# Attention and gated feed-forward on one core: a step's output weights, the next block's queries and a load of h asked for at other places

## The chip, the cores and the metric

The kernel runs on one core of one Trainium2 chip, in one launch. The time is device microseconds (us) of that core, from three runs: 851.23, 847.15 and 847.97, median 847.97. Engines are named as the profile names them: PE (TensorE matmul), PEld (its weight load), DVE (VectorE), ACT (ScalarE), POOL (GpSimd), and SP, which here issues nearly all DMAs from one queue in program order.

## The reference

What is computed is attention within chunks of 64 positions, then a gated feed-forward layer on all tokens:

```python
# q, k, v: (8, 8, 576, 64); chunk 64
scores = scale * np.matmul(q_c, k_c.transpose(0, 1, 2, 4, 3))
scores = scores - np.max(scores, axis=-1, keepdims=True)
attn = np.exp(scores)
attn = attn / (np.sum(attn, axis=-1, keepdims=True) + 1e-09)
out = np.matmul(attn, v_c)
# x: (4608, 512) out of the heads; w_gate, w_val: (512, 1536); w_out: (1536, 512)
g = x @ w_gate
silu = g * (1.0 / (1.0 + np.exp(-g)))
val = x @ w_val
return (silu * val @ w_out).astype(np.float32)
```

All arrays are float32.

## The kernel before

The 4608 tokens are nine blocks of 512 (`N`), and the 1536 inner columns twelve steps of 128 (`NF`). A float32 factor is split into an upper and a lower part, and a product is three matmuls: lower by upper, upper by lower, upper by upper. So a step of one block is 12 matmuls for the gate, 12 for the value, and 12 for the projection with the output weights (`project`, L583 to L585). `lag` puts each projection one step behind, so that its factors (`hh` cast by ACT, `hl` subtracted by DVE, both in `split`, L70 and L71) have a step's time to be made.

The stages that matter here, with their place in the span:

- Up to about 181 us, blocks 0 and 1 go through `first_seven`, which makes the two blocks' gates and values with seven products instead of eight (L915). Block 1's inner values h are kept in HBM for later. Its last call is step 11. After it the next block (`nxt`, the third one) has its scores made, in two halves (L307), and the loads of block 1's h begin (`fetch_h`, L1008).
- From 181 to about 217 us a loop over f projects block 1's steps from what `fetch_h` brings. Beside it goes the third block's attention.
- From 217 to about 325 us a loop over i (twelve steps, f = i + 4 modulo 12) does the third block's feed-forward, with 24 matmuls by `gated` (L505) and 12 by `project` in each step. Beside it, blocks 4 and 5 have their attention done, and six sums of output weights are made, which later blocks use (`WeightSums`): a load of raw weights (`qk_t<-r`, L1403), three POOL subtractions (L1406 to L1408), an ACT cast (L1412), two POOL subtractions (L1415), two stores (`sums<-qk_t`, L1419).
- After that, pairs of blocks.

The order of PE, ACT and DVE is the order of the code (`tc.manual_schedule`), and POOL's is too in the loop over i. So each of these engines stands still until the wait at the head of its queue is over, whatever else would be ready. SP's order is the code's up to the first scores; later a scheduler sets it, which a call `tc.issue_after(x)` holds back until after instruction x. `recent[0]` is the latest load of output weights (`out_again`). The sums' load stands under it:

```python
def sums(self):
    with tc.issue_after(recent[0]):
        nc.sync.dma_start(out=self.raw, in_=kept_raw[self.j].rearrange("p i m -> p (i m)"))
```

`begin_sums(1)` is called at the end of `behind[2]`, that is after step i = 2; `weight_sums[1].split()`, with the ACT cast, stands in `middle[3]`, between step i = 3's gate and value and the cast of its `hh`. What ACT has to do next after that `hh` is to copy the scores of block 4 out of the two PSUM banks of the pool `ps_gv` (L315). The pool has two buffers only: step i = 4's gate and value go to the same two banks.

Of the kernel before, what the change touches and what calls it, by code (L numbers as in the profile page):

```python
# [24 lines left out]
NF = DF // P  # L25
# [8 lines left out]
def attn_then_gated_ffn(ctx: ExitStack, tc: tile.TileContext, qk, v, wgv, wo, out):  # L34
    nc = tc.nc
    const = ctx.enter_context(tc.tile_pool(name="const", bufs=1))
# [7 lines left out]
    ps_gv = ctx.enter_context(tc.tile_pool(name="ps_gv", bufs=2, space=bass.MemoryType.PSUM))  # L44
# [140 lines left out]
    SEVEN, EARLY = 5, 4  # L185
# [29 lines left out]
    def save_w(f):  # L215
        kept_w[f] = store.tile([P, 2, 4 * Q], F32, name=f"w{f}")
        nc.sync.dma_start(out=kept_w[f], in_=w_both[f].bitcast(F32))
# [290 lines left out]
    def out_weights(f, engine=None):  # L508
        both = wp.tile([P, 2, DM], F32R, name="both", tag="wo")
        split(wo_raw[f], both[:, 0], both[:, 1], engine)  # L510
        if f % 2 == 0:
            o = store.tile([P, 2, 2, DM], F32, name=f"o{f}")
            kept_o[f], kept_o[f + 1], two_o[f // 2] = o[:, 0], o[:, 1], o
        out_now[f] = both
        return both[:, 0], both[:, 1]
# [3 lines left out]
    def save_o(f):  # L519
        nc.sync.dma_start(out=kept_o[f], in_=out_now[f].bitcast(F32))  # L520
        if f % 2 == 0:
            kept_raw.append(store.tile([P, 2, DM], F32, name=f"r{f}"))
        nc.sync.dma_start(out=kept_raw[f // 2][:, f % 2], in_=wo_raw[f])
# [3 lines left out]
    def out_again(f, pool=wp, tag="wo"):  # L527
        both = pool.tile([P, 2, DM], F32R, name="both", tag=tag)
        recent[:] = [nc.sync.dma_start(out=both.bitcast(F32), in_=kept_o[f]).ins]
        return both[:, 0], both[:, 1]  # L530
# [87 lines left out]
    def put_off(h):  # L618
        f = len(waiting)
        if f % 2 == 0:  # L620
            kept_h.append(store.tile([P, 2, N], F32, name=f"h{f}"))
        waiting.append(kept_h[-1][:, f % 2])
        nc.scalar.dma_start(out=waiting[f], in_=h)
# [44 lines left out]
    class Product:  # L668
# [4 lines left out]
        def add(self, *which):  # L673
            for w in which:
                self.left -= 1
                some(self.ps, *self.at, [w], first=self.left == 3 * NK - 1, last=not self.left)
# [126 lines left out]
    wo_f = out_weights(0)  # L803
# [56 lines left out]
    for f in range(1, SEVEN):  # L860
# [32 lines left out]
        if f + 1 in (2, SEVEN):  # L893
            quarters = Quarters(f + 1, "w6" if f == 1 else None)
            quarters.sums(w.t)
        up[f + 2].scale()
        wo_f = out_weights(f)
# [12 lines left out]
    def seventh(ps, x, factors, i, first):  # L910
        which, q = FACTORS[i]
        w = [t.rearrange("p (i k m) -> p i k m", i=4, m=P)[:, q] for t in factors[which]]
        for k in range(NK // 2):
            for n, (u, v) in enumerate(((0, 1), (1, 0), (0, 0))):
                nc.tensor.matmul(ps, w[u][:, k], in_turn(x[i][v][:, k]), start=first and k == 0 and n == 0,  # L915
                                 stop=k == NK // 2 - 1 and n == 2, skip_group_check=True)
# [4 lines left out]
    def turns(which):  # L921

        if pending:
            project(*pending[0], which=which)
            if T - 1 in which:
                pending.pop()

    def first_seven(f, done, before):

        o, w = down[f], up[f + 1] if f + 1 < NF else None  # L930
        if f + 2 < NF:
            up[f + 2].load()
        save_o(f - 1)
        done.save()
        if f == NF - 2:
            save_w(EARLY)
            save_w(EARLY + 1)
        factors = (w_both[f][:, 0], w_both[f][:, 1]), done.halves

        def product(ps, i, first):  # L940
            seventh(ps, x_first, factors, i, first)

        ps1 = ps_a.tile([P, N], F32, name="ps_a", tag="ps_a")
        ps2, ps3 = (ps_gv.tile([P, N], F32, name="ps_gv") for _ in range(2))
        h = hp.tile([P, N], F32, name="h")
        v1, v2 = (ld.tile([P, N], F32, name="v", tag="v_t") for _ in range(2))
        product(ps1, 0, True)
        if w:
            w.below()
            w.shift()  # L950
        if f + 1 < NF:
            down[f + 1].load()
        nc.scalar.copy(out=h, in_=ps1)
        o.below()
        if f < NF - 1:
            put_off(before)
        product(ps2, 1, True)
        if w:
            w.join()
            w.upper()  # L960
        nc.scalar.copy(out=v2, in_=ps2)
        turns([0])
        product(ps1, 2, False)
        quarters = Quarters(f + 1)
        if w:
            quarters.sums(w.t)
            w.lower()
        nc.scalar.copy(out=v1, in_=ps1)
        if w:
            quarters.upper()  # L970
        o.shift()
        o.join()
        product(ps3, 3, True)
        add(h, ps3)
        if w:
            quarters.lower()
        nc.scalar.activation(h, h, AF.Silu, scale=2.0 ** -8)
        turns([1])
        product(ps1, 4, False)
        add(v2, ps1)  # L980
        wo_f = out_weights(f, nc.gpsimd)
        product(ps2, 5, False)
        if f + 2 < NF:
            up[f + 2].scale()
        if f + 1 < NF:
            down[f + 1].scale()
        add(v1, ps2)
        times(h, v1)
        p = parts(a0, f, h)
        turns([2])  # L990
        product(ps1, 6, False)
        h2 = const.tile([P, N], F32, name="h2", tag="ts") if f == NF - 2 else hp.tile([P, N], F32, name="h")
        nc.scalar.activation(h2, ps1, AF.Silu, scale=2.0 ** -8)
        turns([3])
        times(h2, v2)
        pending.append((p, wo_f))
        return quarters, h2

    for f in range(SEVEN, NF - 1):
        quarters, h1 = first_seven(f, quarters, h1)  # L1000


    late, last_fetch = [], []

    def fetch_h(i):
        if i < NF // 2 - 1:
            h = ld.tile([P, 2, N], F32, name="h_in", tag="qk_t")
            last_fetch[:] = [nc.sync.dma_start(out=h, in_=kept_h[i]).ins]  # L1008
            late.append(h)
# [9 lines left out]
    def fetch_o(n):  # L1019
        while len(ready_o) < min(n, NF - 2):  # L1020
            f = len(ready_o)
            ready_o.append(out_again(f, const, f"wo{f % 5 - 1}") if f % 5 in (1, 2) else out_again(f))


    nxt = First(2)
    a1.steps = NF - 2, NF - 3
    last_o = pending[0][1]
    _, h2 = first_seven(NF - 1, quarters, None)
    first_qk = [nxt.load_qk(0), nxt.load_qk(1)], [nxt.load_qk(2, 2, const, "turned")]
    fetch_o(2)  # L1030
    nxt.less_top(nxt.products(first_qk[0], ps_gv, "ps_gv"), 0)
    fetch_h(0)
    put = [(parts(a1, NF - 2, h1), last_o)]
    wo_f = pending[0][1]
    lag(None, None)
# [398 lines left out]
    a, pair = nxt, []  # L1434
# [13 lines left out]
    in_order.__enter__()  # L1448
    for f in range(NF):
        lag(*put.pop(0))  # L1450
        fetch_o(f + 3)
        extra.get(f, lambda: None)()
        if f == 7:
            late_sums[EARLY].begin("w3", copied[0])
        elif f == 10:
            late_sums[EARLY].split()
        if f + 2 < NF:
            put.append((prepare(f), ready_o[f]))
        if f == 9:
            with tc.issue_after(recent[0]):  # L1460
                save_w(EARLY + 2)

    pair = pair[0]
    c = pair.a[0]
# [8 lines left out]
    def load_late(a, after):  # L1473
        with tc.issue_after(after):
            load_values(a)
# [12 lines left out]
        with tc.issue_after(weight_sums[3].stored):  # L1488
            scores(a)

    late_queries = []

    def load_second():
        late_queries.append([pair.second().load_qk(0, 2, const, moved(0))])
# [4 lines left out]
    t1, t2 = Turns(c), Turns(None)  # L1499

    def some_of_second(n):
# [4 lines left out]
              4: lambda: pair.a[1].exponents(0, NP), 5: lambda: some_of_second(4), 6: lambda: some_of_second(4),  # L1506
              7: lambda: some_of_second(4)}
    behind = {0: lambda: (c.normalize(0, NP), t1.some(2)), 1: lambda: (load_second(), load_second_too(), t1.some(10)),
              2: lambda: (t1.some(6), load_late(c, pair.a[1].asked)),
              3: lambda: scores(pair.a[1], False, late_queries),  # L1510
              4: lambda: (cross(c, False), pair.a[1].normalize(0, NP)), 5: lambda: some_of_second(10),
              6: lambda: (some_of_second(10), load_late(pair.a[1], weight_sums[2].stored)), 7: lambda: (pair.x0(), pair.x3()),
# [16 lines left out]
    for i in range(NF):  # L1529
        f = (i + EARLY) % NF  # L1530
        h = gated(a, f)
        middle.get(i, lambda: None)()
        wo_f = out_again(f)
        lag(parts(a, f, h), wo_f)
        with tc.issue_after(recent[0]):
            if i in TILES_AGAIN:
                again(TILES_AGAIN.index(i))
            if i in STORED:
                save_w(EARLY + 3 + STORED.index(i))
        if i in SAVED:  # L1540
            late_sums[SAVED[i]].save()
        if i == 4:
            late_sums[0].begin(("ts", "wo0"), pair.a[1].exponentials)
        elif i == 5:
            late_sums[1].begin(moved(5))
        elif i == 6:
            late_sums[1].split()
        behind[i]()
    in_order.__exit__(None, None, None)
    for b in range(3, NB, 2):  # L1550
        pair.last = b + 2 == NB
        middle, beside, behind, bursts, later = {}, {}, {}, {}, {}
        if not pair.last:
            n = Pair(b + 2, moved(11))
            c = n.a[0]
            bursts = {0: lambda: late_scores(c), 3: lambda: scores(n.second()), 8: lambda: cross(c), 10: lambda: cross(n.a[1])}
            middle = {2: lambda: c.exponents(0, NP), 5: lambda: n.a[1].exponents(0, NP), 10: lambda: load_late(n.a[1], asked_left[0]), 11: lambda: (n.s1(), n.s4())}
            t1, t2 = Turns(c), Turns(None)
# [19 lines left out]
        if not pair.last:  # L1578
            pair = n
# [34 lines left out]
```

## Time and profile before

| | before |
|---|---|
| median of three runs | 847.97 us |
| the profiled execution, its own time | 848.97 us |
| its span, first to last instruction | 847.2 us |
| PE busy | 829.5 us, 98% |
| DVE, ACT, POOL busy | 606.3, 433.6, 161.8 us |
| DMA, mean over the span | 273 GB/s |
| mean granted TensorE clock | 0.999 |

Busy time of an engine counts its instructions alone, not what it waits for. With PE busy 98% of the span, some 17.7 us are left in which it is not; which of them a change can reach is read from PE's waits in the stretch in question. A share of the whole span says little on such a stretch. A DMA's time runs from its issue to its landing, and holds what it waits behind in the queue.

### The profile page before, as it was taken

What the parts mean: (1) busy time and instruction counts of PE and PEld (TensorE: products, weight loads), DVE (VectorE), ACT (ScalarE), POOL (GpSimd) and SP (SyncE); (2) the same over time, 40 slices, a digit from 0 to 9 for tenths busy, and PEclk for the clock granted to TensorE, in tenths of its full rate; (3) what the DMA queues carried; (4) which work ended last, traced back from release to release, by engine and by line L of the source; (5) the groups of instructions that cost most, each with busy time, mean ns of one, the idle gap of its engine ahead of it and who ended that gap; (6) DMA issues with size and microseconds to landing.
All of it is one profiled execution on the core that took longest, in us unless ns stands there. A gap on an engine that the chain in (4) does not pass through costs nothing.

```text
span 847.2 us, 16691 instructions
## 1 busy us (share of the span) xinstructions
PE 829.5 (98%) x6689; PEld 742.8 (88%) x6689; DVE 606.3 (72%) x946; ACT 433.6 (51%) x650; POOL 161.8 (19%) x118
## 2 busy tenths in 40 slices
PE   7999999999999999999999999999999999999997
PEld 6788888878887888888889998888889988888997
DVE  5898988854798956568886976678768943333475
ACT  4876889753625345535335743553337533333353
POOL 1300001102155742233110001413010002222100
PEclk9999999999999999999999999999999999999999
DMA  9698788899999899866678779666768576666643
GB/s 351 250 337 310 291 297 315 322 336 303 411 326 360 298 406 373 299 212 227 234 256 303 265 231 335 233 209 227 233 208 298 163 259 231 230 227 226 241 173 114
DMA packets 96654, 231.27 MB, mean 273 GB/s; under 512 B 32064, under 2 KB 58176, under 8 KB 83904
## 3 DMA queue, kind: packets, MB, share of 16 engines
q1 hardware_dynamic: 94848, 227.31, 75.3%
q10 hardware_dynamic: 1728, 2.88, 1.1%
q8 instruction: 53, 0.87, 0.4%
q14 instruction: 25, 0.20, 0.1%
HBM read 177.21 MB, written 52.95 MB: 272 GB/s over the span
## 4 chain that ended last, share of the span: by engine, by line
PE 86%; DMA 7%; POOL 2%; DVE 2%; ACT 1%; issue 1%; SPq 0%; DVEq 0%; ACTq 0%; POOLq 0%
PE ps_a L915 26%; PE ps_gv L915 19%; PE ps_o L571 14%; PE ps_gv L505 10%; PE ps_gv L571 6%; DMA v_t<-in_v 3%; PE ps_o L583 2%; PE ps_o L584 2%; PE ps_o L585 2%; PE ps_a L307 2%; DMA qk_t<-r 1%; PE ps_a L395 1%; DMA h_in<-h 1%; DMA both<-o 1%; POOL qk_t L1406 1%
## 5 line engine op out<-in xcount | busy, mean ns | idle before, releaser
L915 PE MATMUL ps_a<-x,factors 128*128 128x512 f32 x864 | 211.1, 380 | 0.4 <-issue 0.4
L915 PEld LDWEIGHTS ps_a<-x,factors 128*128 128x128 f32 x864 | 154.3, 190 | 18.1 <-issue 1.1
L915 PE MATMUL ps_gv<-x,factors 128*128 128x512 f32 x648 | 157.6, 379 | 0.1
L915 PEld LDWEIGHTS ps_gv<-x,factors 128*128 128x128 f32 x648 | 122.3, 189 | 17.9 <-PE ps_a L915 0.4
L1240 POOL TENSOR_TENSOR kept<-kept 128x512 f32<-128x512 f32 x39 | 57.0, 1460 | 362.8 <-DVE kept L555 358.5
L505 PE MATMUL ps_gv<-xh,w 128*128 128x512 f32 x352 | 103.3, 380 | 0.0
L382 DVE STREAM_TRANSPOSE turned<-s_sb 32x256 f32<-32x256 f32 x192 | 83.7, 436 | 3.1
L70 ACT CAST hh<-kept 128x512 fp32r<-128x512 f32 x111 | 67.2, 617 | 28.7 <-PE ps_o L571 15.4
L505 PEld LDWEIGHTS ps_gv<-xh,w 128*128 128x128 f32 x352 | 66.4, 189 | 9.4 <-ACT xh L660 0.2
L1214 ACT ACTIVATE kept<-ps_a 128x512 f32<-128x512 f32 x36 | 21.5, 598 | 89.7 <-PE ps_a L915 89.3
L505 PE MATMUL ps_gv<-xl,w 128*128 128x512 f32 x176 | 65.6, 383 | 1.1 <-issue 1.1
L919 DVE TENSOR_TENSOR kept<-kept,ps_gv 128x512 f32<-128x512 f32 x30 | 20.6, 688 | 63.7 <-PE ps_gv L915 63.4
L71 DVE TENSOR_TENSOR hl<-kept,hh 128x512 fp32r<-128x512 f32 x84 | 57.3, 687 | 12.4 <-ACT hh L70 12.0
L555 DVE SCALAR_TENSOR_TENSOR kept<-v,kept 128x512 f32<-128x512 f32 x66 | 45.7, 693 | 24.2 <-ACT kept L1214 17.6
L571 PE MATMUL ps_o<-sums,hh 128*128 128x256 f32 x504 | 62.7, 275 | 0.0
L571 PEld LDWEIGHTS ps_o<-sums,hh 128*128 128x128 f32 x504 | 59.3, 192 | 0.4 <-DVE hh L71 0.4
L583 PE MATMUL ps_o<-both,hl 128*128 128x512 f32 x144 | 55.3, 384 | 2.2 <-DVE hl L71 1.5
L571 PEld LDWEIGHTS ps_o<-both,hh 128*128 128x128 f32 x288 | 51.4, 189 | 6.8
L584 PE MATMUL ps_o<-both,hh 128*128 128x512 f32 x144 | 54.6, 379 | 0.0
L585 PE MATMUL ps_o<-both,hh 128*128 128x512 f32 x144 | 54.6, 379 | 0.0
L571 PE MATMUL ps_o<-both,hh 128*128 128x256 f32 x288 | 53.5, 276 | 0.0
L919 DVE TENSOR_TENSOR v<-v,ps_a 128x512 f32<-128x512 f32 x43 | 29.5, 687 | 22.0 <-PE ps_a L915 20.6
(164 smaller groups left out, 1447.2 us busy)
## 6 DMA issues: line engine op xcount, KB each, us to landing
factors<-w SPq DMA_DIRECT2D x36, 1024.0 KB, 4.8
factors<-t SPq DMA_DIRECT2D x36, 1024.0 KB, 6.7
sums<-sums SPq DMA_DIRECT2D x36, 512.0 KB, 5.8
w<-w SPq DMA_DIRECT2D x16, 1024.0 KB, 10.1
t<-th SPq DMA_DIRECT2D x24, 512.0 KB, 5.0
raw<-in_wgv SPq DMA_DIRECT2D x11, 1024.0 KB, 8.8
both<-o SPq DMA_DIRECT2D x22, 512.0 KB, 9.1
qk_t<-in_qk SPq DMA_DIRECT2D x10, 1024.0 KB, 10.5
```

Source lines behind the costliest of these rows:

```text
L70: nc.scalar.copy(out=hi, in_=src)
L71: (engine or nc.vector).tensor_tensor(out=lo, in0=src, in1=hi.bitcast(F32), op=ALU.subtract)
L382: nc.vector.transpose(out=self.turned[to:to + 32, p:p + 2, j, :, 32 * (i % 2):32 * (i % 2) + 32], in_=src[32 * i:32 * i + 32, :, o // 2, 3 ...
L505: nc.tensor.matmul(ps, w, in_turn(x), start=first and (k, i) == which[0], stop=last and (k, i) == which[-1])
L555: nc.vector.scalar_tensor_tensor(out=h, in0=pv, scalar=2.0 ** -8, in1=h, op0=ALU.mult, op1=ALU.mult)
L571: nc.tensor.matmul(banks[t // 2][:, t % 2], h[u][:, t * P:(t + 1) * P], in_turn(w[v]), start=first and t % 2 == 0 and n == 0, stop=n == 2, ...
L583: nc.tensor.matmul(o, hl[:, ts], woh, start=f == a.steps[0], stop=False)
L584: nc.tensor.matmul(o, hh[:, ts], wol, start=False, stop=False)
L585: nc.tensor.matmul(o, hh[:, ts], woh, start=False, stop=f == a.steps[1])
L915: nc.tensor.matmul(ps, w[u][:, k], in_turn(x[i][v][:, k]), start=first and k == 0 and n == 0, stop=k == NK // 2 - 1 and n == 2, skip_group ...
L919: nc.vector.tensor_tensor(out=t, in0=t, in1=ps, op=ALU.add)
L1240: engine.tensor_tensor(out=out, in0=one, in1=two, op=op)
```

## The change

Three things move. In the last call of `first_seven` the last two quarters of a projection go together, then come the first half of the third block's scores with their subtraction of the maxima, and then the last of the seven products; the issue of `fetch_h(0)` stands behind the scores there, and the third output-weight load of the next loop is told to go after it. And in the loop over i, `out_again(7)` is asked for at the end of step i = 2, ahead of the values' loads of `load_late`, instead of in step i = 3.

```diff
-    def first_seven(f, done, before):
+    def first_seven(f, done, before, amid=None):
...
-        turns([2])
+        turns([2] if amid is None else [2, 3])
+        if amid:
+            amid()
         product(ps1, 6, False)
         h2 = const.tile([P, N], F32, name="h2", tag="ts") if f == NF - 2 else hp.tile([P, N], F32, name="h")
         nc.scalar.activation(h2, ps1, AF.Silu, scale=2.0 ** -8)
-        turns([3])
+        if amid is None:
+            turns([3])
         times(h2, v2)
         pending.append((p, wo_f))
         return quarters, h2
...
-    _, h2 = first_seven(NF - 1, quarters, None)
-    first_qk = [nxt.load_qk(0), nxt.load_qk(1)], [nxt.load_qk(2, 2, const, "turned")]
-    fetch_o(2)
-    nxt.less_top(nxt.products(first_qk[0], ps_gv, "ps_gv"), 0)
-    fetch_h(0)
+    first_qk, first_h = [], []
+
+    def first_scores():
+        first_qk.extend(([nxt.load_qk(0), nxt.load_qk(1)], [nxt.load_qk(2, 2, const, "turned")]))
+        fetch_o(2)
+        first_qk.append(nxt.products(first_qk[0], ps_gv, "ps_gv"))
+        fetch_h(0)
+        first_h.extend(last_fetch)
+        nxt.less_top(first_qk[2], 0)
+
+    _, h2 = first_seven(NF - 1, quarters, None, first_scores)
...
         lag(*put.pop(0))
-        fetch_o(f + 3)
+        with tc.issue_after(first_h[0]):
+            fetch_o(f + 3)
...
-    late_queries = []
+    late_queries, sooner = [], []
...
-              2: lambda: (t1.some(6), load_late(c, pair.a[1].asked)),
+              2: lambda: (t1.some(6), sooner.append(out_again(EARLY + 3)), load_late(c, pair.a[1].asked)),
...
         middle.get(i, lambda: None)()
-        wo_f = out_again(f)
+        wo_f = sooner.pop() if sooner else out_again(f)
```

In what is built, ACT and POOL keep their order row for row. On PE and DVE only the last call of `first_seven` differs. On PE, near 175 us of the span, before (`L915` are the seven products, `L583` to `L585` a quarter of a projection, `L307` scores):

```order
L583 MATMUL ps_o<-both,hl 128x512
L584 MATMUL ps_o<-both,hh 128x512
L585 MATMUL ps_o<-both,hh 128x512
L915 MATMUL ps_a<-xl_105,th 128x512
L915 MATMUL ps_a<-xh_104,th 128x512 x2
L915 MATMUL ps_a<-xl_105,th 128x512
L915 MATMUL ps_a<-xh_104,th 128x512 x2
L583 MATMUL ps_o<-both,hl 128x512
L584 MATMUL ps_o<-both,hh 128x512
L585 MATMUL ps_o<-both,hh 128x512
L307 MATMUL ps_a<-qk_t 64x64 x32
```

and now:

```order
L583 MATMUL ps_o<-both,hl 128x512
L584 MATMUL ps_o<-both,hh 128x512
L585 MATMUL ps_o<-both,hh 128x512
L307 MATMUL ps_a<-qk_t 64x64 x32
L915 MATMUL ps_a<-xl_105,th 128x512
L915 MATMUL ps_a<-xh_104,th 128x512 x2
L915 MATMUL ps_a<-xl_105,th 128x512
L915 MATMUL ps_a<-xh_104,th 128x512 x2
```

The scores and the quarter ahead of them pass the six matmuls of the last product.

On SP, the DMAs issued behind the store of step 11's output weights (`o_1790<-both`), before:

```order
L529 DMA both<-o_711 128x1024 x2
L520 DMA o_1790<-both 128x1024
L529 DMA both<-o_891 128x1024
L1008 DMA h_in<-h_734 128x1024
L600 DMA out<-o_sb 64x2x512 x4
L1008 DMA h_in<-h_962 128x1024
```

and now, nine lines further down in the file:

```order
L529 DMA both<-o_711 128x1024 x2
L520 DMA o_1790<-both 128x1024
L1011 DMA h_in<-h_734 128x1024
L529 DMA both<-o_891 128x1024
L600 DMA out<-o_sb 64x2x512 x4
L1011 DMA h_in<-h_962 128x1024
```

The first load of h and a load of output weights change places.

On SP again, near 232 to 255 us of the span, around the values' loads `v_t<-in_v` of block 4; `r_938` are the raw weights of the second of the six sums, `o_1350` holds step 7's output weights, `w_830` and `w_940` are weights for steps of i = 10 and 11. Before, the beginning and the end of this piece:

```order
L1469 DMA w<-w_830 128x2048
L1403 DMA qk_t<-r_938 128x1024
L1419 DMA sums<-qk_t 512x1x256
L279 DMA qk_t<-in_qk 128x2x1024
L287 DMA v_t<-in_v 128x4x64
L289 DMA v_t<-in_v 64x4x64
L1419 DMA sums<-qk_t 512x1x256
L289 DMA v_t<-in_v 64x4x64
```

```order
L287 DMA v_t<-in_v 128x4x64
L289 DMA v_t<-in_v 64x4x64 x2
L529 DMA both<-o_1350 128x1024
L1469 DMA w<-w_940 128x2048
L529 DMA both<-o_1568 128x1024
```

and now, from the second store of sums on:

```order
L1428 DMA sums<-qk_t 512x1x256
L289 DMA v_t<-in_v 64x4x64
L529 DMA both<-o_1350 128x1024
L287 DMA v_t<-in_v 128x4x64
L289 DMA v_t<-in_v 64x4x64 x2
L287 DMA v_t<-in_v 128x4x64
L289 DMA v_t<-in_v 64x4x64 x2
L287 DMA v_t<-in_v 128x4x64
L289 DMA v_t<-in_v 64x4x64 x2
L1412 DMA qk_t<-r_938 128x1024
L1479 DMA w<-w_940 128x2048
```

Step 7's output weights have come ahead of three of the four groups of values' loads. The raw weights `r_938` have gone from ahead of the first store of sums to behind the last of the values' loads: `recent[0]`, behind which they are held, is now the load of step 7's output weights. The next raw weights, `r_1166`, have gone behind one more pair of a load and a store in the same way.

## Rows read from the trace of the kernel before

**Rows 1.** The page's first part: busy us, share of the span, and number of instructions of each engine.

```profile
PE 829.5 (98%) x6689; PEld 742.8 (88%) x6689; DVE 606.3 (72%) x946; ACT 433.6 (51%) x650; POOL 161.8 (19%) x118
```

**Rows 2.** All that PE waited for from 160 to 310 us: us in total, how often, the longest.

```profile
PE ps_o L583 <- DVE hl L71: 1.5, 1, 1.5
PE ps_gv L505 <- issue: 1.1, 1, 1.1
PE ps_a L395 <- issue: 1.1, 1, 1.1
PE ps_o L583 <- DMA both<-o: 0.7, 1, 0.7
```

**Rows 3.** Instructions in order of time from 174 to 190 us: start, us, engine, line, operation, and in brackets the idle time before and what ended it. PE, SP, ACT and DVE.

```profile
174.92 0.38 PE L915 MATMUL ps_a<-xl,th 128*128 128x512 f32 x1
...
176.95 1.16 PE L307 MATMUL ps_a<-qk_t 64*64 64x64 f32 x64
...
178.88 0.32 SPq L529 DMA_DIRECT2D both<-o  x1
...
179.29 0.41 SPq L1008 DMA_DIRECT2D h_in<-h  x1
...
186.99 0.38 PE L585 MATMUL ps_o<-both,hh 128*128 128x512 f32 x1
187.51 0.62 ACT L70 CAST hh<-h_in 128x512 fp32r<-128x512 f32 x1 [3.10 <-DMA h_in<-h]
...
188.16 0.69 DVE L71 TENSOR_TENSOR hl<-h_in,hh 128x512 fp32r<-128x512 f32 x1 [3.00 <-ACT hh L70]
...
188.91 0.48 PE L583 MATMUL ps_o<-both,hl 128*128 128x512 f32 x1 [1.54 <-DVE hl L71]
```

**Rows 4.** The load of output weights issued at 178.88: KB, and us from issue to landing.

```profile
both<-o SPq DMA_DIRECT2D x1, 512.0 KB, 7.3
```

**Rows 5.** The chain that ended last, in order of time, from 179 to 209 us: start, us, what.

```profile
179.29 8.12 DMA h_in<-h
...
194.37 0.02 issue
194.39 5.37 DMA both<-o
...
199.77 8.27 DMA v_t<-in_v
208.04 0.04 issue
208.08 1.14 PE ps_a L495 x58
```

**Rows 6.** SP's issues in order of time from 235 to 255 us: start, us, line, what.

```profile
235.60 0.32 SPq L1403 DMA_DIRECT2D qk_t<-r  x1
...
239.72 3.55 SPq L1419 DMA_DIRECT2D sums<-qk_t  x1
243.31 2.54 SPq L289 DMA_DIRECT2D v_t<-in_v  x1
...
246.21 0.38 SPq L287 DMA_DIRECT2D v_t<-in_v  x1
...
251.99 1.93 SPq L289 DMA_DIRECT2D v_t<-in_v  x2
254.01 0.55 SPq L529 DMA_DIRECT2D both<-o  x1
```

**Rows 7.** The DMAs issued at 235.60 and at 254.01: KB, and us from issue to landing.

```profile
qk_t<-r SPq DMA_DIRECT2D x1, 512.0 KB, 9.2
...
both<-o SPq DMA_DIRECT2D x1, 512.0 KB, 4.6
```

**Rows 8.** Two stretches: busy us of PE, PEld, DVE, ACT, POOL (and number of instructions), granted PE clock, DMA share, GB/s.

```profile
232.00:244.00 12.00, 12.00 (x57) 10.52 (x56) 10.73 (x21) 2.33 (x4) 5.82 (x5) 1.00 1.02 381
250.00:256.00 6.00, 6.00 (x148) 5.17 (x147) 5.83 (x11) 2.09 (x4) 2.52 (x2) 1.00 0.63 149
```

**Rows 9.** From 244 to 256 us, first POOL's and ACT's instructions in order of time, then two of PE's; columns as in rows 3.

```profile
244.97 1.27 POOL L1406 TENSOR_TENSOR qk_t<-qk_t 128x512 f32<-128x512 f32 x1 [5.28 <-DMA qk_t<-r]
246.32 1.06 POOL L1407 TENSOR_TENSOR qk_t<-qk_t 128x256 f32<-128x256 f32 x1
247.46 0.74 POOL L1408 TENSOR_TENSOR qk_t<-qk_t 128x256 f32<-128x256 f32 x1
...
248.23 1.05 ACT L1412 CAST qk_t<-qk_t 128x1024 fp32r<-128x1024 f32 x1 [2.03 <-POOL qk_t L1408]
250.27 0.62 ACT L70 CAST hh<-h 128x512 fp32r<-128x512 f32 x1 [0.99 <-DVE h L555]
251.83 1.07 ACT L315 COPY s_sb<-ps_a 128x512 f32<-128x512 f32 x2 [0.95 <-PE ps_a L307]
255.60 0.60 ACT L548 ACTIVATE h<-ps_gv 128x512 f32<-128x512 f32 x1 [2.69 <-PE ps_gv L505]
...
250.62 2.09 PE L307 MATMUL ps_a<-qk_t 64*64 64x64 f32 x128
252.65 0.48 PE L505 MATMUL ps_gv<-xl,w 128*128 128x512 f32 x1
```

**Rows 10.** The chain that ended last, from 256 to 270 us, and a step's gate and value in it from 219 us.

```profile
219.41 5.38 PE ps_gv L505 x24
...
256.27 11.62 DMA qk_t<-r
```

**Rows 11.** The opening in stretches of 2 us, columns as in rows 8.

```profile
6.00:8.00 2.00, 0.94 (x29) 0.63 (x20) 1.51 (x4) 0.00 (x0) 0.00 (x0) 1.00 0.96 305
...
12.00:14.00 2.00, 0.92 (x14) 0.64 (x6) 1.80 (x3) 1.23 (x2) 1.90 (x1) 1.00 1.02 407
```

## The prediction

> **What bounds the kernel now.** I began with the page's busy times: PE is busy 98% of the span [rows 1], so what is to be gained is only what PE waits for, and what is to be lost is any new wait of PE. Of the third block's stretch I then read PE's waits [rows 2]: four, 4.4 us in all. Two of them are what the change goes at. The 1.5 us behind DVE's `hl` is the first projection out of `h_in`: PE had done the work before it at 186.99 + 0.38 = 187.37 and went on at 188.91; the subtraction waited for the cast, the cast for the load of h, which took 8.12 us and landed at 187.41 [rows 3, 5]. The 0.7 us behind `both<-o` is step 7's output weights, asked for at 254.01 and landed 4.6 us later [rows 2, 6, 7]. The two waits put down to "issue" have no releaser in the trace, and I leave them as they are. Then I read, for every instruction that the change moves past another on SP, who waits for that other one, and there is the main term.
>
> The sum is made against the profiled execution's own 848.97 us (span 847.2); the median of the three runs is 847.97, 1.0 lower, and I give times against this.
>
> **The scores and the load of h.** No instruction is added. On PE the 64 recorded score matmuls (1.16 us) pass the six of the seventh product (174.92 to 176.21); the work between 174 and 178 is the same in both orders. In the new order they would start where the quarter ahead of them ends, near 175.6, and end near 176.7. The load of h waits for them, and no longer for the load of output weights that was issued at 178.88 ahead of it; it is then issued near 176.8 instead of 179.29 [rows 3]. It takes the place of that load in the queue, which landed 7.3 us after its issue, at 186.2 [rows 4]. With the cast's 0.62, the subtraction's 0.69 and 0.1 between them, PE's factor is there by 187.6 at the latest, 0.2 after PE wants it. So 1.3 of 1.54 us go. Bounds: a gain of 1.5, if the load lands sooner still, and none, if the next wait takes it up. The nearest one: the third block's columns are held up until 208.04 by values' loads, issued at 199.77. That issue waited for a load of output weights which was issued at 194.39, as PE's projection ended [rows 5]; PE's being earlier makes it earlier too. I take a gain of 1.2. The scores' side costs nothing that I can find: the activation of the last product comes some 1.5 us later, and what needs it on PE is the projection of step 11 of block 1, which has eight quarters of other projections ahead of it as cover; without that cover it would cost those 1.5.
>
> **Step 7's output weights.** They pass three groups of values' loads, whose last issue ended at 253.92 [rows 6], so they land long before 258.7. The wait of 0.7 goes. Bounds: 0 and 0.7; I take 0.7. The values they pass come one issue (0.55) later, and nothing wants these for several us more.
>
> **The second sum's raw weights.** This is what the third edit brings along. Before, the raw weights were issued at 235.60, landed 9.2 us later, and POOL made its three subtractions from 244.97 to 248.20; ACT's cast, which stands in ACT's queue ahead of step 3's `hh` and of the copies out of `ps_gv`, had waited 2.03 us for them and ran at 248.23 [rows 6, 7, 9]. The slack was gone even then: the copies ran at 251.83, and PE began the next gate at 252.65, as its scores ended, in the two banks that the copies had emptied [rows 9]. Now the raw weights are issued behind the last of the values' loads, where step 7's output weights stood at 254.01. The queue ahead of that place holds 512 KB less of raw weights, and 512 KB more of output weights with an issue of 0.55. The DMA engines were full from 232 to 244 (share 1.02, 381 GB/s [rows 8]), so taking 512 KB out brings what follows 512 / 381 = 1.3 us forward. I put the issue at 254.0 - 1.3 + 0.55 = 253.3. From 250 to 256 the engines were at 0.63 [rows 8], so the landing takes what `both<-o` of the same size took from there, 4.6 [rows 7]: 257.9. From the landing to PE's going on: 0.1 to POOL's start, 3.2 for its three subtractions (244.97 to 248.20), ACT's cast 1.05, `hh` 0.62, and half of the two copies' 1.07 [rows 9], 5.5 in all. So PE would start step 4's gate at 263.4 instead of 252.65, a wait of 10.7 us. (PE's being 1.2 earlier moves both sides alike, since the first store of sums, behind which these DMAs stand, follows on ACT and PE.)
>
> PE has no cover for it: in its queue, behind the gate, stand the value, the projection of step 3, whose `hh` is held up by the same cast, and the columns. DVE stands at the subtraction of that `hh`. So the 10.7 us are added whole. What comes later in the loop is released by these same engines: the code lets the exponentials on ACT start POOL's next sums. It moves along with PE, so I expect neither a second wait nor a recovery.
>
> Bounds. From below: SP gets its eleven issues, from 243.27 on (239.72 + 3.55), done in 0.55 each, and the raw weights are issued at 249.3, land at 253.9, and PE waits 6.8. From above: they meet a full queue as the raw weights issued at 256.27 did, which took 11.62 [rows 10]; PE waits 17.7. The row at 254.01 is the nearest, at the same place in the same queue, so I stay with 10.7.
>
> **PE's clock.** [...] No row has PE idle for as long as 10 us. [...] I take 2.0, nearer the lower end, where the opening's rows are.
>
> [...]
>
> **The sum.** -1.2 - 0.7 + 10.7 + 2.0 = +10.8 us; 848.97 becomes 859.8, and 847.97 becomes 858.8.
>
> **The rivals.**
> - The clock keeps its upper level: 858.8 - 2.0 = 856.8. For it: the clock of 1.00 all through the opening. Against: the wait is several times as long as any there.
> [...]
> - The load of h does not bring PE forward, and the edit does not do what it says: 858.8 + 1.2 = 860.0. For it: the queue was full as h was loaded, and the columns have a wait of their own right behind.
> - SP is quicker and PE waits 6.8, with the clock up: 847.97 - 1.9 + 6.8 = 852.9. For it: 0.63 of DMA share at the end of the piece. Against: SP's own rows, 1.93 for a pair of issues.
> - The raw weights meet a full queue, and PE waits 17.7: 865.8. Against: the big weights' load is behind them, not ahead.
> - Not slower: the raw weights are there in time for the cast, and the two gains stand alone, 847.97 - 1.9 = 846.1. It is decided at one point: they must land by 252.65 - 5.5 = 247.1, so by their best landing of 4.6 be issued by 242.5. Against it: SP was held at the second store of sums until 243.27, and the values stand between.
>
> **How the numbers follow.** The forecast, 858.8, has 0.50; the clock kept up 0.15; no gain from h 0.12; the quick SP 0.07; the full queue 0.05; the clock down for a step 0.05; not slower 0.06. The range 853 to 864 leaves out the last three, and the quick SP's lower half, under 2 in 10. About 0.5% (4.2 us) is what a measurement of this kernel can tell from no change. Every case but the last is slower by more than that (852.9 only just), 0.94; of the last, 846.1 is within it, 0.04, and I give 0.02 to its coming out faster than I can account for.
>
> **What would show it.** In the profile after: the load of h issued near 175.6 to 177, and PE's first projection out of `h_in` with a wait under 0.5; no wait of PE for `both<-o` near 258; the raw weights' issue as the last behind the values' loads, near 252; POOL's subtraction (L1415 there) waiting some 14 us longer for `qk_t<-r`; ACT's cast (L1421) waiting over 10 us for POOL; and PE at a gate's first matmul waiting about 10.7 us for ACT's copies of the scores. Beside it, a granted clock under 1.00 in the stretch that follows, or not. Wrong I am if ACT's cast finds POOL done, or if the raw weights are issued before 245; and the sum is wrong if the later sums' casts hold PE up a second time.

## The result and the profile after

| | before | after |
|---|---|---|
| median, runs in turn on one chip (8 each) | 850.01 us | 854.01 us |
| the profiled execution, its own time | 848.97 us | 852.81 us |
| its span | 847.2 us | 851.0 us |
| PE busy | 829.5 us | 831.0 us |
| mean granted TensorE clock | 0.999 | 0.993 |

The change is slower: ratio 1.0058, with an interval of 1.0040 to 1.0076. That is +4.0 us between the medians and +3.84 between the two profiled executions, against a forecast of +10.8. The sign and the mechanism came out as forecast; of the size hardly two fifths came.

In the changed file L1008 is L1011, L1403 to L1419 are L1412 to L1428, and L1469 is L1479: three, nine and ten lines further down.

All that PE waited for from 160 to 310 us stands now in one row. The four of [rows 2] are gone, the two "issue" waits too, which the prediction had left as they were:

```profile
PE ps_gv L505 <- ACT s_sb L315: 7.8, 1, 7.8
```

SP's issues around the values' loads, to lay beside [rows 6]:

```profile
237.19 0.60 SPq L1428 DMA_DIRECT2D sums<-qk_t  x1
237.84 2.77 SPq L289 DMA_DIRECT2D v_t<-in_v  x1
240.71 0.55 SPq L529 DMA_DIRECT2D both<-o  x1
...
246.31 0.80 SPq L287 DMA_DIRECT2D v_t<-in_v  x1
247.29 1.26 SPq L289 DMA_DIRECT2D v_t<-in_v  x2
248.59 0.60 SPq L1412 DMA_DIRECT2D qk_t<-r  x1
249.24 1.44 SPq L1479 DMA_DIRECT2D w<-w  x1
```

The raw weights are the last behind the values' loads, at 248.59. The second store of sums, which held SP for 3.55 us in [rows 6], is through in 0.60. Then POOL, ACT and PE, which answer to [rows 9]; the bracket says how long the engine had been idle and for what:

```profile
252.82 1.26 POOL L1415 TENSOR_TENSOR qk_t<-qk_t 128x512 f32<-128x512 f32 x1 [15.78 <-DMA qk_t<-r]
254.16 0.72 POOL L1416 TENSOR_TENSOR qk_t<-qk_t 128x256 f32<-128x256 f32 x1
254.96 0.72 POOL L1417 TENSOR_TENSOR qk_t<-qk_t 128x256 f32<-128x256 f32 x1
...
255.72 1.04 ACT L1421 CAST qk_t<-qk_t 128x1024 fp32r<-128x1024 f32 x1 [12.17 <-POOL qk_t L1417]
256.67 0.61 ACT L70 CAST hh<-h 128x512 fp32r<-128x512 f32 x1
257.19 1.07 ACT L315 COPY s_sb<-ps_a 128x512 f32<-128x512 f32 x2
...
247.97 2.09 PE L307 MATMUL ps_a<-qk_t 64*64 64x64 f32 x128
257.82 0.79 PE L505 MATMUL ps_gv<-xl,w 128*128 128x512 f32 x1 [7.76 <-ACT s_sb L315]
```

These have to be read from the bottom up: PE, done with block 4's scores, stands 7.76 us for ACT's copies; the copies stand in ACT's queue behind the cast; the cast has stood 12.17 for POOL, and POOL 15.78 for the load. The chain of waits says the same in order of time, and shows what held SP:

```profile
240.71 6.56 DMA both<-o
247.27 0.02 issue
247.29 0.60 SPq L289
...
248.59 4.10 DMA qk_t<-r
...
257.28 0.49 ACT s_sb L315
257.78 0.04 issue
257.82 6.39 PE ps_gv L505 x17
```

The raw weights took 4.10 us to land. Ahead of that, SP's issue at 247.29 went out 0.02 us after `both<-o` had landed, so the load that was brought forward is itself a link of the chain. It held SP for 0.2 us only: SP's issue before that one had ended at 246.31 + 0.80 = 247.11, and SP's own issues fill nearly all of the 6.56.

The stretch in windows of 4 us, columns as in [rows 8]:

```profile
248.00:252.00 4.00, 2.06 (x129) 1.93 (x128) 1.68 (x4) 0.00 (x0) 0.00 (x0) 1.00 0.79 221
252.00:256.00 4.00, 0.00 (x0) 0.00 (x0) 0.00 (x0) 0.28 (x1) 2.71 (x3) 0.57 0.90 285
256.00:260.00 4.00, 2.18 (x5) 1.82 (x6) 2.65 (x3) 2.26 (x4) 2.95 (x2) 0.50 0.96 356
260.00:264.00 4.00, 4.00 (x13) 3.23 (x13) 3.90 (x7) 0.75 (x2) 0.00 (x0) 0.65 1.02 426
264.00:268.00 4.00, 4.00 (x20) 3.42 (x19) 1.41 (x3) 3.55 (x3) 0.88 (x1) 1.00 0.93 344
```

The granted clock, 1.00 all through this stretch before, is 0.50 from 256 to 260 and back at 1.00 from 264. The gate and value that begin at 257.82 end at 265.56: 7.74 us for what takes 5.38 at a clock of 1.00 [rows 10], so 2.36 for the clock (`L583` is the projection behind the value):

```profile
265.56 0.38 PE L583 MATMUL ps_o<-both,hl 128*128 128x512 f32 x1
```

The first projection out of `h_in` has no wait left, and the load of h was issued at 175.71, against 179.29 in [rows 3].

### The profile page after: what moved, and what is told of

Read it like the earlier page. It is cut to its first block, busy times and chain, and to the rows that moved or that the text cites. A ratio compares the mean times of both kernels' runs of the same rounds, so it can differ in the third digit from the quotient of the medians.

```text
span 851.0 us, 16689 instructions
## 1 busy us (share of the span) xinstructions
PE 831.0 (98%) x6689; PEld 745.2 (88%) x6689; DVE 606.8 (71%) x946; ACT 433.3 (51%) x650; POOL 162.6 (19%) x118
## 4 chain that ended last, share of the span: by engine, by line
PE 91%; DMA 4%; DVE 2%; ACT 1%; SPq 1%; POOL 1%; issue 0%; DVEq 0%; POOLq 0%; ACTq 0%
PE ps_a L915 26%; PE ps_gv L915 19%; PE ps_o L571 14%; PE ps_gv L505 12%; PE ps_gv L571 6%; PE ps_o L583 3%; PE ps_o L584 3%; PE ps_o L585 3%; DMA v_t<-in_v 2%; PE ps_a L307 1%; PE ps_a L395 1%; DMA both<-o 1%; SPq L289 1%; DMA qk_t<-in_qk 1%; DMA qk_t<-r 0%; PE ps_a L495 0%
## 5 line engine op out<-in xcount | busy, mean ns | idle before, releaser
L915 PE MATMUL ps_a<-x,factors 128*128 128x512 f32 x864 | 210.7, 380 | 0.9 <-ACT v L1204 0.7
L915 PEld LDWEIGHTS ps_a<-x,factors 128*128 128x128 f32 x864 | 154.4, 190 | 18.3 <-issue 1.2
L915 PE MATMUL ps_gv<-x,factors 128*128 128x512 f32 x648 | 157.6, 379 | 0.1
L915 PEld LDWEIGHTS ps_gv<-x,factors 128*128 128x128 f32 x648 | 122.2, 189 | 17.9 <-PE ps_a L915 0.4
L583 PE MATMUL ps_o<-both,hl 128*128 128x512 f32 x144 | 55.0, 382 | 0.0
L585 PE MATMUL ps_o<-both,hh 128*128 128x512 f32 x144 | 54.6, 379 | 0.0
L71 DVE TENSOR_TENSOR hl<-h,hh 128x512 fp32r<-128x512 f32 x38 | 31.6, 831 | 23.2 <-ACT hh L70 22.1
```

The lines of the kernel that those rows point to most:

```text
L71: (engine or nc.vector).tensor_tensor(out=lo, in0=src, in1=hi.bitcast(F32), op=ALU.subtract)
L583: nc.tensor.matmul(o, hl[:, ts], woh, start=f == a.steps[0], stop=False)
L585: nc.tensor.matmul(o, hh[:, ts], woh, start=False, stop=f == a.steps[1])
```

## The experiments

"Before" in each is the kernel before, run in turn on the same chip. An offset is the start of a PE row less the start of the same row in the profile of before; the change's own offsets are -0.70 us at 34 us, -2.51 at 199, -2.65 at 251, +6.70 at 262, +5.33 at 296, +3.55 at 335 and +3.84 at 623.

**The two halves of the change.** The edits near 175 us alone (`out_again(7)` back in step 3):

```diff
-              2: lambda: (t1.some(6), sooner.append(out_again(EARLY + 3)), load_late(c, pair.a[1].asked)),
+              2: lambda: (t1.some(6), load_late(c, pair.a[1].asked)),
...
-        wo_f = sooner.pop() if sooner else out_again(f)
+        wo_f = out_again(f)
```

> The two edits around 175 us alone; step 7's output weights and the second sum's raw weights stand on SP as before the change. Theory (the loss is all from the place of the second sum's raw weights, the front edits gain 1.5 to 1.8): PE has no wait for ACT's copies of the scores near 250, the 1.5 us wait near 189 is gone, the 0.7 for both<-o near 256 is still there, the clock stays at 1.00, and the time is 1.0 to 2.0 us under the kernel before. Rival (the scores ahead of the seventh product, or the changed order of loads, cost later): 2 to 4 us above the kernel before.

Measured: 848.1 us, ratio 0.9981 [0.9962, 1.0000]. No wait near 189 us, none for ACT's copies. One thing is against the expectation: PE waits 2.3 us for "issue" near 298, and the granted clock, expected at 1.00, is 0.79 from 296 to 300.

And the loop's edit alone, on the kernel before:

```diff
-    late_queries = []
+    late_queries, sooner = [], []
...
-              2: lambda: (t1.some(6), load_late(c, pair.a[1].asked)),
+              2: lambda: (t1.some(6), sooner.append(out_again(EARLY + 3)), load_late(c, pair.a[1].asked)),
...
-        wo_f = out_again(f)
+        wo_f = sooner.pop() if sooner else out_again(f)
```

> Only the edit that asks for step 7's output weights among the values' loads. Theory: the raw weights come behind the values' loads, PE waits 7 to 9 us for ACT's copies, the granted clock is near 0.5 for the first matmuls after it, and the time is 5 to 7 us above the kernel before. Rival (the loss needs both edits): within 1.5 us of the kernel before.

Measured: 856.67 us, ratio 1.0091 [1.0057, 1.0125], a wait of 8.9 us for ACT's copies, the clock at 0.50 from 256 to 264. All of the loss is in this edit.

```profile
PE ps_gv L505 <- ACT s_sb L315: 8.9, 1, 8.9
```

The profile shows one thing more: the old order near 175 us is in it, and the wait on `hl` of [rows 2, 3] is not. The cast of what the load of h brings is 2.6 us earlier than in [rows 3]:

```profile
177.58 0.32 SPq L529 DMA_DIRECT2D both<-o  x1
177.99 0.43 SPq L1008 DMA_DIRECT2D h_in<-h  x1
...
184.91 0.62 ACT L70 CAST hh<-h_in 128x512 fp32r<-128x512 f32 x1 [0.86 <-DMA h_in<-h]
```

Its second store of sums, with the raw weights gone from ahead of it, is as short as in the changed kernel:

```profile
238.78 0.58 SPq L1419 DMA_DIRECT2D sums<-qk_t  x1
```

**Is it the raw weights' place?** The whole change, but the second sum's raw weights are held behind what they stood behind before (the held version):

```diff
-        def sums(self):
-            with tc.issue_after(recent[0]):
+        def sums(self, after):
+            with tc.issue_after(after):
...
-        weight_sums[j].sums()
+        weight_sums[j].sums(held.pop() if held else recent[0])
...
-              2: lambda: (t1.some(6), sooner.append(...
+              2: lambda: (t1.some(6), held.append(recent[0]), sooner.append(...
```

> All of the change, but the second sum's raw weights are held behind the load of step 6's output weights as before, so that they are issued ahead of the first store of sums again; step 7's output weights still come ahead of three groups of values. Theory (the place of the raw weights is the whole loss): no wait of PE for ACT's copies, none for both<-o near 256, none of 1.5 near 189, clock 1.00, and 1.7 to 2.7 us under the kernel before. Rival (the output weights among the values' loads cost by themselves, since the SP queue behind them is late): a wait over 1 us stays between 245 and 300, and the time is at or above the kernel before.

Measured: 847.62 us, ratio 0.9981 [0.9962, 1.0000]. The same kernel in more rounds:

> The version with the second sum's raw weights held back to their place before, with all the rest of the change, in more rounds. If the rest of the change is a gain, the ratio is under 1 with its interval (0.997 to 0.999 by the run before, 847.6); if what it showed was chance, the interval holds 1. The changed kernel was at 1.0058, so its whole loss is the raw weights' place if this one is not above 1.0.

Measured: 847.58 us, ratio 0.9982 [0.9966, 0.9998]. And the same edit without those near 175 us:

> The kernel before with the loop's edit alone and the raw weights held in their place: only step 7's output weights pass three groups of values' loads. By the sum: the wait of 0.7 us on them goes, so 0.7 us under the kernel before (0.999), and the version with the front edits as well is lower by what those are worth (1.2 by the sum; about 0 if the wait near 189 us is one execution's). If a load that goes ahead of the values' loads costs somewhere else, this one is at 1.000 or above.

Measured: 848.38 us, ratio 0.9993 [0.9974, 1.0012]. With the raw weights' place in SP's queue put back, the +4.0 us become -1.5: that place is the whole loss. (The third sum's raw weights come back with them, behind one pair of loads of `both` and `w` instead of two; no wait of PE stands on these in either version.) The profile of the held version's second run has the raw weights at 232.78 and the second store of sums holding SP again:

```profile
232.78 0.32 SPq L1412 DMA_DIRECT2D qk_t<-r  x1
...
236.90 3.45 SPq L1428 DMA_DIRECT2D sums<-qk_t  x1
```

All that PE waits for from 160 to 320 us in this run is one row, and in windows its clock dips behind it:

```profile
PE ps_gv L505 <- issue: 2.9, 1, 2.9
```

```profile
256.00:260.00 4.00, 4.00 (x138) 3.44 (x137) 2.11 (x3) 3.30 (x5) 1.32 (x1) 1.00 0.91 293
260.00:264.00 4.00, 1.10 (x5) 0.77 (x5) 3.97 (x3) 1.06 (x3) 3.76 (x4) 0.96 1.01 398
264.00:268.00 4.00, 4.00 (x13) 3.25 (x12) 3.01 (x3) 1.65 (x2) 2.76 (x2) 0.62 1.07 419
```

The step's gate and value, with that wait inside, take 10.03 us:

```profile
259.72 0.48 PE L505 MATMUL ps_gv<-xl,w 128*128 128x512 f32 x1
...
269.75 0.38 PE L583 MATMUL ps_o<-both,hl 128*128 128x512 f32 x1
```

Without the 5.38 that they take at a clock of 1.00 and the wait of 2.90, 1.75 are left for the clock. So part of what the rest of the change wins is given back here: PE, 3.9 us ahead of before's profile at 262 us, is 0.5 ahead at 296. This version is faster than both kernels, by little. How its 1.5 us divide between the load of h and step 7's output weights stays open: 0.9982, 0.9993 and 0.9981 are not apart by their intervals.

**The issue's time or the landing's?** The change with the raw weights issued right behind step 7's output weights, ahead of the three groups of values' loads:

```diff
-... sooner.append(out_again(EARLY + 3)), load_late(...
+... sooner.append(out_again(EARLY + 3)), begin_sums(1), load_late(...
...
-        if j:
+        if j > 1:
```

> The changed kernel with the second sum's raw weights issued right behind step 7's output weights, ahead of three groups of values' loads instead of behind them; by the changed kernel's trace that is some 7.3 us sooner (near 241.3 instead of 248.6). Theory (PE's wait follows the raw weights' landing): they land 1.3 us behind those output weights, which took 6.6 us there, so near 248.6 instead of 252.7, and PE's wait for ACT's copies falls from 7.8 to 3 to 4.5 us; less of it is met at the lower clock, and the time is 4 to 6 us under the changed kernel, so 0.5 under to 1 above the kernel before. Rival (the wait follows the issue): the wait falls by the whole 7.3, to about 0.5. Rival (the place does not matter): 7 to 9 us as in the changed kernel.

Measured: 849.97 us, ratio 1.0013 [0.9998, 1.0029], 1.3 us above before, and a wait for the copies of 5.1 us, both a little more than expected:

```profile
PE ps_gv L505 <- ACT s_sb L315: 5.1, 1, 5.1
```

```profile
242.20 0.54 SPq L529 DMA_DIRECT2D both<-o  x1
243.11 0.34 SPq L1412 DMA_DIRECT2D qk_t<-r  x1
...
250.22 1.26 POOL L1415 TENSOR_TENSOR qk_t<-qk_t 128x512 f32<-128x512 f32 x1 [12.87 <-DMA qk_t<-r]
```

Issued 5.5 us sooner than in the change, the raw weights reached POOL only 2.6 sooner, since 7.1 us lay between their issue and POOL's start (250.22 - 243.11) where it had been 4.2 (252.82 - 248.59); PE's wait is 2.7 shorter. So what PE paid here went by the landing, and the place nearer the front of the queue was worth less than the issues that it passed.

**Is the clock's fall the wait's doing?** First with PE kept at work by the second half of block 4's scores, made six more times (the results are the same):

```diff
+            for _ in range(again):
+                for k in range(2):
+                    a.scores(tiles[1][0][:, k], k, ps[1])
...
-              3: lambda: scores(pair.a[1], False, late_queries),
+              3: lambda: scores(pair.a[1], False, late_queries, 6),
```

> The changed kernel, in which PE makes the second half of block 4's scores six times more into the same bank, about 6.5 us of small matmuls in the place of its wait; the result is the same. Theory (after the wait the clock falls because PE stood idle, and that costs 2.4 us: step 4's gate and value took 7.7 us against 5.4): PE goes on at the same point, the granted clock stays 1.00, gate and value take 5.4, and the time is 2 to 3 us under the changed kernel, so 1 to 2.5 above the kernel before. Rival (the clock falls for another reason, or those 2.4 us are hidden behind other engines later): gate and value slow again, or the time within 1 us of the changed kernel.

Measured: 862.79 us, ratio 1.0165 [1.0131, 1.0200]. That is 9 us above the change, not 2 to 3 under it. PE did not work through: it stood 8.3 us in three waits that the profile puts down to "issue" (4.38, 1.38 and, by the difference, 2.5, near 266).

```profile
249.63 2.72 PE L307 MATMUL ps_a<-qk_t 64*64 64x64 f32 x169
253.73 2.09 PE L307 MATMUL ps_a<-qk_t 64*64 64x64 f32 x128 [1.38 <-issue]
260.20 3.61 PE L307 MATMUL ps_a<-qk_t 64*64 64x64 f32 x128 [4.38 <-issue]
```

The clock fell again, to 0.57 from 260 to 264, so this run says nothing on the question. Then with 32 large matmuls between the two halves of the scores, whose results are thrown away:

```diff
+            for _ in range(filler):
+                nc.tensor.matmul(ps[0].rearrange("p n c k -> p (n c k)"), w_hi[7][:, 0, 0],
+                                 in_turn(nxt.x[0][0][:, 0]), start=True, stop=True)
...
-              3: lambda: scores(pair.a[1], False, late_queries),
+              3: lambda: scores(pair.a[1], False, late_queries, 32),
```

> The changed kernel with 32 matmuls of 128x512 (6.9 us at 0.216) between the two halves of block 4's scores, into the bank that the second half then overwrites, so that PE works through most of its wait with few instructions; the result is the same. Theory (the clock falls because PE stands idle, and the lower clock costs 2.4 us): PE goes on at the same point as in the changed kernel, the granted clock stays 1.00, step 4's gate and value take 5.4 instead of 7.7 us, and the time is 1.5 to 2.5 us under the changed kernel. Rival (those 2.4 us are hidden behind other engines later): gate and value take 5.4, but the time is within 0.7 us of the changed kernel. Rival (extra instructions starve PE as in the kernel with the small matmuls): waits put down to issue, and a longer time.

Measured: 852.28 us, ratio 1.0046 [1.0029, 1.0063]. The filler was too short: PE still stood 2.86 us for the copies, the clock was at 0.50 from 260 to 264, and gate and value took 268.29 - 260.08 = 8.21 us. With 52 of them:

> The changed kernel with 52 matmuls of 128x512 (results thrown away) between the two halves of block 4's scores, where the earlier one had 32. At the 0.224 us that each of those 32 took, PE works some 4.5 us longer there and reaches the gate about when the copies of the scores are done, with a wait for them under 0.5 us. Theory: the fall of the clock in the changed kernel comes from PE's standing, so here the granted clock stays at 1.00 and the stretch from the gate's first matmul to the value's last (48 matmuls at 4.5 to 5.4 us a gate) takes about 5.4 us, not the 7.74 of the changed kernel; by the offsets the loss is then 52 x 0.224 = 11.6 us less the slack that it fills, near 7.8 + 1.5, and no clock term beside it. Rival: the clock falls in this stretch for the work that runs there, whether PE stands or not; then the stretch is again near 7.7 us.

Measured: 853.55 us, ratio 1.0058 [1.0037, 1.0078]. Here POOL waits for the load as in the change, but PE never stands, and the windows have the clock at 1.00 throughout:

```profile
254.19 1.27 POOL L1418 TENSOR_TENSOR qk_t<-qk_t 128x512 f32<-128x512 f32 x1 [16.07 <-DMA qk_t<-r]
...
250.14 11.49 PE L297 MATMUL ps_a<-xh,w 128*128 128x512 f32 x52
261.56 1.16 PE L310 MATMUL ps_a<-qk_t 64*64 64x64 f32 x64
262.65 0.48 PE L508 MATMUL ps_gv<-xl,w 128*128 128x512 f32 x1
...
267.93 0.38 PE L586 MATMUL ps_o<-both,hl 128*128 128x512 f32 x1
```

```profile
256.00:260.00 4.00, 4.00 (x21) 3.49 (x20) 1.28 (x1) 2.54 (x4) 2.76 (x4) 1.00 0.90 296
260.00:264.00 4.00, 4.00 (x78) 3.33 (x77) 3.90 (x7) 0.00 (x0) 1.22 (x1) 1.00 1.01 420
264.00:268.00 4.00, 4.00 (x20) 3.49 (x20) 1.71 (x3) 2.37 (x3) 0.00 (x0) 1.00 1.00 389
```

From the gate's first row to the value's end it is 267.93 - 262.65 = 5.28 us, not 7.74. The rival, that the clock falls for the work in this stretch, is out; the fall is the standing's. PE is 9.1 us behind before's profile at 262 us, near the 9.3 expected, but 6.0 behind at 623, and the medians differ by 4.1. And 11.5 us of work that nobody needs cost this kernel no more than the change's 7.76 us of standing with the clock's fall behind it: both have 1.0058.

**How much is one execution's?** The kernel before and the changed one, each profiled a second time:

> The kernel before, once more, for its waits. Theory (the 1.5 us wait near 189 depends on how the load of h lands in an execution, since the kernel with the back edit alone, which has the old order there, did not have it): a wait there between 0 and 1.5 us, and not 1.54 again; the two waits put down to issue between 260 and 300 are there again, at 0.5 to 2.5 us each, and the one for both<-o near 258 at 0.4 to 0.9. Rival (the old order always waits): 1.3 to 1.7 near 189.

Measured: 847.06 us. PE waits for `both<-o` 1.3 us, more than expected, and for "issue" 1.3 and 1.0; near 189 us for nothing.

> The changed kernel, once more, for its waits. [...] Rival (the missing issue waits were chance): 0.5 to 2 us of them.

Measured: 854.42 us, with 8.8 us for the copies and the clock at 0.50 from 256 to 260. One "issue" wait of 0.6 us is left, near 304. Between these two executions the change costs 7.4 us, between the first two 3.8.

## Why the prediction was right, and where it was off

The working of the forecast against the two profiled executions:

| term | forecast | measured | from |
|---|---|---|---|
| the opening, which the change doesn't touch | 0 | -0.7 | offset at 34 us |
| load of h and scores | -1.2 | -1.8 | offsets at 34 and 199 |
| step 7's output weights | -0.7 | -0.7 | the wait is gone |
| PE's wait for ACT's copies | +10.7 | +7.8 | PE's waits |
| clock | +2.0 | +2.4 | 7.74 less 5.38 |
| behind the stretch | 0 | -2.9 | offsets at 262 and 623 |
| not assigned | | -0.2 | |
| sum | +10.8 | +3.8 (by times) | |

**The second sum's raw weights** were the right term, and the waits on POOL, ACT and PE came in the forecast order. Its size was off by 2.9 us, and 2.1 of these are in one step: "I put the issue at 254.0 - 1.3 + 0.55 = 253.3". In before's time (2.65 later) the issue came at 248.59 + 2.65 = 251.2. I had let SP go on from the second store of sums when it did before, at 243.27. But that store's 3.55 us were of the load that the change takes away from ahead of it: the store takes 0.60 in the profile after, 0.58 with the loop's edit alone, and 3.45 again where the raw weights are held in their old place. So SP went on at 237.84 + 2.65 = 240.5, 2.8 sooner than I had it; the eleven issues then took 248.59 - 237.84 = 10.75, a little more than my 10.0. The 1.3 us that I entered for 512 KB less in the queue was the smaller part of what their going freed. The landing took 4.1, not 4.6, and from there to PE's going on it was 257.82 - 252.69 = 5.1, not 5.5: 0.9 less in the two together. The two other profiles of this order show 8.9 and 8.8, so the first is at the low end of what it costs. The held version shows this term to be the whole loss.

**The clock** fell, as the forecast had it and the first rival had not. The 2.0 of the sum was my estimate, and no run shows that term: no row of before has PE idle for long. What the runs showed in its place is 2.36 us behind the wait of 7.76: with the clock at 0.50 the gate took 5.15 us (257.82 to 262.97), and the value, with the clock at 1.00 again from 263, took 2.59. So it was down for the gate, not for a whole step. That the standing brought it down is shown by the run with 52 matmuls in the place of the wait, where it stays at 1.00.

**"So I expect neither a second wait nor a recovery"** is the step that failed outright, with 2.9 us. I had left the two "issue" waits of [rows 2] alone because nothing in the trace releases them. In the profile after they are not there: PE, late by then, no longer runs into them, and the offset falls by 1.37 between 262 and 296 and by 1.78 between 296 and 335, each where one of these waits (1.1 and 1.1) had stood. The waits make up 2.2 of these 3.15; where the other 0.9 come from is not shown. The other late profiles give back as much at the same two places (1.41 and 1.78 with the loop's edit alone, 1.42 and 1.73 with 52 filler matmuls), and the change's second profile, with 0.6 of "issue" wait left at the second place, 1.41 and 0.93. The held version shows the other side: with PE early, the wait at the gate is 2.0 and 2.9. So in these profiles the waits took up part of a lead and gave part of a delay back. Their cause stays open: they stand behind 128 matmuls of 64x64 while the DMA share is near 1.0, and the run with more such matmuls had 8.3 us of them, but in the profile after the same 128 matmuls run from 301.60 on, at a DMA share of 1.06, with no wait behind them.

**The load of h.** The direction was right, the reason only half: the 1.54 us of [rows 3] belonged to that execution. Of three other profiles with the old order near 175 us two have no such wait and are about as early at 199 us as the change (-2.17 and -2.46 to its -2.51); in the third it is 0.6. So the 1.2 us were not there to be had each time; what the edits near 175 us give is not told apart from nothing by the interval of the run with these edits alone (up to 1.0000).

**Step 7's output weights** came as forecast: no wait for them near 258 in the profile after, 0.7 to 1.3 in those of before. **The rival on the other side**, raw weights in time for the cast, did not come; the held version makes it true by force, and is 1.5 us under before where that case had 1.9.

**The range** held 854.01 near its low end. The forecast stood against 847.97, the median of the three runs shown; the eight runs of before beside the changed kernel had 850.01, 2.0 more. So the miss is better read from the differences: +10.8 forecast, +4.0 measured. Put as differences from 847.97 the range ran from +5.0 to +16.0, and +4.0 lies under it: that 854.01 fell into the range is owed to those 2.0 us, and is luck.

## What to carry over

Before a load is moved ahead in a queue, look for what is told to go "behind the last one asked for": such an order moves along with the load, and takes with it both a third transfer's landing and the hold that this transfer put on the queue (here a landing at 252.7 instead of 244.8, and the 3.55 us of one store). What an in-order engine waits for cost by its landing here, through every step to the engine that sets the end, and the wait of TensorE cost its clock too: 2.4 us behind one of 7.8, and 1.75 behind one of 2.9. Before a gain is entered for a wait of about 1 us, see whether it stands in more than one execution (the 1.54 us of before's first profile were nothing in its second), and count "issue" waits behind a delay as time that may come back (2.2 us here).

## What the runs showed of the hardware

- The granted clock fell behind PE's waits. In windows of 4 us its lowest was 0.50 behind the waits of 8.9 (the loop's edit alone), 8.8 and 7.8 (the change) and 2.9 us (32 filler matmuls), 0.62 behind 5.1 (the raw weights issued between) and behind 2.9 (held version, second run), 0.66 behind 2.0 (its first run) and 0.79 behind 2.3 (the edits near 175 us alone). In windows of 1 us of the change's profile it was 1.00 up to 252, 2 us into the wait, 0.79 from 252 to 253, 0.50 from 253 to 262, and 1.00 again from 263, 5 us after PE had gone on. It stayed at 1.00 behind the waits of 1.5, 1.1 and 1.1 us in the profile of before, and behind those of 1.3 (for `both<-o`) and 1.0 in its second one.
- What the lower clock cost the gate and value behind the wait did not grow with the wait: 2.8 us with 32 filler matmuls (8.21 less 5.38) behind a wait of 2.9, 1.75 in the held version behind the other wait of 2.9, 2.4 in the change behind 7.8.
- 384 more matmuls of 64x64 in the place of PE's wait (169, 128 and 128 recorded rows from 249.63 to 263.81 us, where the change has 128 in all) brought 8.3 us of "issue" waits; 52 of 128x512 brought none.
- The second store of sums held SP for 3.55 and 4.04 us in the two profiles of before, 3.45 in the held version's second and 2.69 with the loop's edit and the raw weights held, all with the raw weights ahead of it; without them for 0.60 and 0.66 in the two of the change, 0.58 with the loop's edit alone and 0.60 with the raw weights issued between.
- The same 512 KB load (`r_938`) from the same queue landed in 4.1 us behind the values' loads and in 9.2 us from its place before; ahead of three groups of them POOL started on it 7.1 us after its issue.
